# Weight conversion moved off GpSimd, first-group squares on ScalarE, natural rows for w_in: a linear-attention and feed-forward kernel on one core

## The chip, the cores and the metric

The kernel runs on one core of a Trainium2 chip. The core has five engines that work side by side and wait for each other by semaphores: TensorE (PE, matrix products, with its weight loads shown as PEld), VectorE (DVE), ScalarE (ACT), GpSimd (POOL) and SyncE (SP), which here only issues DMAs. The metric is the time of one execution in device microseconds (us), as the median of several runs.

## The reference

Four batches of eight heads, 768 steps, head size 48. A state of 48x48 per head decays and takes up an outer product at each step; the rows of the result, all heads side by side, then go through a feed-forward block.

```python
for t in range(S):                       # (B, H, S, D) = (4, 8, 768, 48)
    state = alpha[:, :, t, :, None] * state + einsum('bhd,bhe->bhde', k[:, :, t], v[:, :, t])
    y[:, :, t] = einsum('bhd,bhde->bhe', q[:, :, t], state)
x = y.transpose(0, 2, 1, 3).reshape(B * S, H * D)      # 3072 x 384
h = np.maximum(x @ w_in, 0.0)                          # w_in 384 x 2048
out = (h * h) @ w_out                                  # w_out 2048 x 384
```

q, k, v and alpha are fp32. w_in and w_out come as 64-bit floats, two 32-bit words each, and become fp32 on the chip, by bit operations on the words.

## The kernel before

The tokens are cut into 24 blocks of 128 steps (six chunks of four batches). The attention of a block has four stages, named in the code: `decays` (transposes of alpha on PE, logarithm on ACT, running sum on DVE, two exponentials on ACT), `turn` (q and k transposed and scaled), `scores` (q times k per head, masked by DVE; k turned back), and `values` (state update, and y in PSUM). Every four blocks make a group of 512 tokens. Its y lands in a tile xT of 3 x 128 rows, model dimension on the partitions, which is read by the feed-forward part: `ffn_in` makes one of 16 hidden slices of 128 (three steps over xT, relu on ACT, square on DVE), `ffn_out` adds two hidden slices into the output tile of one block (PE), and copies the tile out at the end.

The order of all instructions is written by hand: each engine takes its own in the order of the code. First comes a prelude, the attention of blocks 0 to 3. Then, for each group g, there are 16 slots; a slot holds one attention stage of the blocks of group g+1 and the next units of feed-forward work of group g, two `ffn_in` units in each of the first eight slots, four `ffn_out` units in each of the last eight. So the attention of the next group runs between the matmuls of this one. Group 5 has no attention beside it.

The weights come in 16 pieces of 128 x 768 (eight of w_in, eight of w_out), through three raw tiles. `next_weights`, called three times in the prelude and once or twice a slot in group 0, converts one piece and issues the load of another. A piece takes one ACT instruction (L133), five on DVE (L134 to L149) and two on POOL (L152, L153). The state product is also on POOL (L283).

The head size 48 is not a divisor of 128. So the heads lie in pairs, at partitions 0 to 47 and 64 to 111 of four tiles. Before, xT keeps that layout for three of the four pairs, and the last pair goes into the gaps (partitions 48 to 63 and 112 to 127) by six small DMAs (L296), and w_in is loaded with its rows in the same arrangement, by four DMAs a piece on SP's and ACT's queues (L113, L114).

SP and ACT issue their DMAs in program order, and an issue waits for a semaphore that an earlier DMA still holds; there are eight, used in turn.

Of the kernel before, what the change touches and what calls it, by code (L numbers as in the profile page):

```python
# [8 lines left out]
FP32 = mybir.dt.float32  # L9
U32 = mybir.dt.uint32  # L10
AF = mybir.ActivationFunctionType
ALU = mybir.AluOpType
PSUM = bass.MemoryType.PSUM
# [6 lines left out]
def kernel(  # L20
# [30 lines left out]
    NJ = DF // 128  # L51
    G = 64 - D
    NR = 3
    assert S % C == 0 and H * D == DM and NP == KM + 1 and KM * G == D and NBLK % GB == 0

    consts = ctx.enter_context(tc.tile_pool(name="consts", bufs=1))
    raw_pool = ctx.enter_context(tc.tile_pool(name="raw", bufs=NR))
# [2 lines left out]
    p2 = ctx.enter_context(tc.tile_pool(name="p2", bufs=2))  # L60
    x_pool = ctx.enter_context(tc.tile_pool(name="x", bufs=2))
    ps_att = ctx.enter_context(tc.tile_pool(name="ps_att", bufs=4, space=PSUM))
    ps_h = ctx.enter_context(tc.tile_pool(name="ps_h", bufs=2, space=PSUM))
    ps_o = ctx.enter_context(tc.tile_pool(name="ps_o", bufs=2, space=PSUM))
    ctx.enter_context(tc.manual_schedule())


# [35 lines left out]
    def load_weights(i):  # L103
        dst = (w_in + w_out)[i]
        dt = moe_w_in.dtype
        raw = dst if dt == FP32 else raw_pool.tile(list(dst.shape), dt, tag="raw", name="raw")
        raws[i] = raw
        if i < NW:
            src = moe_w_in[:, i * DF // NW : (i + 1) * DF // NW]
            own = src[0 : 2 * KM * D].rearrange("(k e r) f -> r e k f", e=2, r=D)  # L110
            gap = src[2 * KM * D : DM].rearrange("(e k r) f -> r e k f", e=2, r=G)
            for e, dma in enumerate((nc.sync, nc.scalar)):
                dma.dma_start(out=raw[64 * e : 64 * e + D], in_=own[:, e])  # L113
                dma.dma_start(out=raw[64 * e + D : 64 * e + 64], in_=gap[:, e])  # L114
        else:
            i -= NW
            src = moe_w_out[i * DF // NW : (i + 1) * DF // NW, :]
            nc.sync.dma_start(out=raw, in_=src.rearrange("(j r) m -> r j m", r=128))

    def convert_weights(i):  # L120

        if moe_w_in.dtype == FP32:
            return
        w = (w_in + w_out)[i].rearrange("a k f -> a (k f)")
        n = w.shape[1]
        words = raws.pop(i).rearrange("a k f -> a (k f)").bitcast(U32)
        words = words.rearrange("a (n h) -> a n h", h=2)
        lo, hi = words[:, :, 0], words[:, :, 1]  # L130
        mag = cv_pool.tile([128, n], U32, tag="mag", name="mag")
        cut = cv_pool.tile([128, n], U32, tag="cut", name="cut")
        nc.scalar.activation(out=w, in_=lo, func=AF.Copy, scale=2.0**-52)  # L133
        nc.vector.tensor_scalar(  # L134
            out=mag, in0=hi, scalar1=1, scalar2=None, op0=ALU.logical_shift_left
        )
        nc.vector.tensor_scalar(  # L137
            out=cut, in0=hi, scalar1=3, scalar2=0x3FFFFFF8,
            op0=ALU.logical_shift_left, op1=ALU.bitwise_and,
        )  # L140
        nc.vector.scalar_tensor_tensor(  # L141
            out=cut, in0=hi, scalar=0xC0000000, in1=cut,
            op0=ALU.bitwise_and, op1=ALU.bitwise_or,
        )
        nc.vector.scalar_tensor_tensor(  # L145
            out=cut.bitcast(FP32), in0=mag, scalar=float(897 << 21), in1=cut.bitcast(FP32),
            op0=ALU.is_ge, op1=ALU.mult,
        )
        nc.vector.tensor_scalar(  # L149
            out=mag, in0=cut, scalar1=0xFF800000, scalar2=None, op0=ALU.bitwise_and  # L150
        )
        nc.gpsimd.tensor_tensor(out=w, in0=w, in1=mag.bitcast(FP32), op=ALU.mult)  # L152
        nc.gpsimd.tensor_tensor(out=w, in0=w, in1=cut.bitcast(FP32), op=ALU.add)  # L153

    for n in range(NIN):
        load(n)
    to_load, to_convert = list(range(2 * NW)), list(range(2 * NW))

    def next_weights():
        if to_convert:  # L160
            convert_weights(to_convert.pop(0))
        if to_load:
            load_weights(to_load.pop(0))


# [5 lines left out]
    again = consts.tile([128, NP, C], FP32, name="again")  # L171
    nc.vector.memset(again, 1.0)
    nc.vector.memset(again[:, :, 0:1], 0.0)
    NAM = 2
    am_t = kept("am", NAM, [128, 2, NP, 128])
    for t in am_t:
# [62 lines left out]
    def values(n):  # L239
        c, batch = divmod(n, B)  # L240
        qT = qkT.pop(n)[0]
        b = bs.pop(n)
        v_in = tiles["v"][n % NV]
        am = am_t[n % NAM]
        st = s_t[batch]
        kv = None
        if c < NCH - 1:
            kv = ps_att.tile([128, NP, 2 * D], FP32, tag="att", name="kv")
            kt = ks.pop(n)
            for p in range(NP):  # L250
                nc.tensor.matmul(  # L251
                    out=kv[:, p, :], lhsT=kt[:, p, :],
                    rhs=v_in[:, 2 * p * D : 2 * (p + 1) * D], start=True, stop=True,
                )
            sm = p2.tile([128, NP, D], FP32, tag="sm", name="sm")
            for e in range(2):
                rows = slice(64 * e, 64 * e + D)
                new = kv[rows, :, e * D : (e + 1) * D]
                if c == 0:
                    nc.vector.tensor_copy(out=sm[rows], in_=new)  # L260
                else:
                    nc.vector.tensor_tensor(  # L262
                        out=sm[rows], in0=new, in1=st[rows, :, 64 * e : 64 * e + D], op=ALU.add
                    )

        y = ps_att.tile([128, NP, C], FP32, tag="att", name="y")
        if c:
            for p in range(NP):
                nc.tensor.matmul(  # L269
                    out=y[:, p, :], lhsT=st[:, p, :], rhs=qT[:, p, :],  # L270
                    start=(p == 0), stop=False, skip_group_check=True,
                )
        for p in range(NP):
            for e in range(2):
                nc.tensor.matmul(  # L275
                    out=y[64 * e : 64 * e + 64, p, :], lhsT=v_in[:, (2 * p + e) * D : (2 * p + e) * D + 64],
                    rhs=am[:, e, p, :], start=(c == 0 and p == 0), stop=True,
                    skip_group_check=True,
                )
        if kv is not None:  # L280
            for e in range(2):
                rows = slice(64 * e, 64 * e + D)
                nc.gpsimd.tensor_tensor(  # L283
                    out=st[rows, :, 64 * e : 64 * e + D], in0=sm[rows],
                    in1=b[rows, :, C - 1 : C].to_broadcast([D, NP, D]), op=ALU.mult,
                )
        g, t = divmod(n, GB)
        if t == 0:
            xT[g] = x_pool.tile([128, KM, GB * C], FP32, tag="xT", name="xT")
        x = xT[g][:, :, t * C : (t + 1) * C]  # L290
        yg = p2.tile([128, C], FP32, tag="yg", name="yg")
        nc.scalar.activation(out=yg, in_=y[:, KM, :], func=AF.Copy)  # L292
        nc.scalar.activation(out=x, in_=y[:, 0:KM, :], func=AF.Copy)
        for e in range(2):
            for kk in range(KM):
                nc.sync.dma_start(  # L296
                    out=x[64 * e + D : 64 * e + 64, kk, :],
                    in_=yg[64 * e + G * kk : 64 * e + G * (kk + 1), :],
                )


    hid, acc = {}, {}

    def ffn_in(g, j):
        hid[j] = hid_pool.tile([128, GB * C], FP32, tag="hid", name="hid")
        w, c0 = w_in[j * NW // NJ], j % (NJ // NW) * 128
        ps = ps_h.tile([128, GB * C], FP32, tag="h", name="h")
        for kk in range(KM):
            nc.tensor.matmul(  # L309
                out=ps, lhsT=w[:, kk, c0 : c0 + 128], rhs=xT[g][:, kk, :],  # L310
                start=(kk == 0), stop=(kk == KM - 1),
            )
        r = p2.tile([128, GB * C], FP32, tag="r", name="r")
        nc.scalar.activation(out=r, in_=ps, func=AF.Relu)  # L314
        nc.vector.tensor_tensor(out=hid[j], in0=r, in1=r, op=ALU.mult)  # L315

    def ffn_out(g, t, i):
        per = NJ // NW
        if i == 0:
            acc[t] = ps_o.tile([128, 512], FP32, tag="o", name="o")  # L320
        for j in range(per * i, per * (i + 1)):
            nc.tensor.matmul(  # L322
                out=acc[t][:, 0:DM],
# [19 lines left out]
    for n, s in order:  # L343
# [5 lines left out]
        if s == 3 and n + NV == GB:  # L349
            load(n + NV)  # L350
            load_weights(to_load.pop(0))
        if n == GB - 1 and s > 0:
            next_weights()

    NS = GB * len(stages)
    for g in range(NBLK // GB):
        units = [(ffn_in, (g, j)) for j in range(NJ)]
        units += [(ffn_out, (g, t, i)) for t in range(GB) for i in range(NW)]
        cost = {ffn_in: KM * GB * C, ffn_out: NJ // NW * DM}
        total = sum(cost[f] for f, _ in units)  # L360
        done = 0
        for slot in range(NS):
            i, s = divmod(slot, len(stages))
            n = (g + 1) * GB + i
            if n < NBLK:
                stages[s](n)
            for _ in range(1 + s % 2):
                next_weights()
            if s == 0 and n + 1 < NBLK:
                load(n + 1)  # L370
            while units and done * NS < total * (slot + 1):
# [33 lines left out]
```

## Time and profile before

| | |
|---|---|
| median of 3 runs | 722.15 us (721.2 to 723.8) |
| the profiled execution, its span | 723.61 us, 721.8 us |
| PE busy | 659.7 us (91%) |
| PE weight load | 387.0 us (54%) |
| DVE busy | 268.7 us (37%) |
| ACT busy | 149.5 us (21%) |
| POOL busy | 92.3 us (13%) |
| granted PE clock, mean | 0.955 |

Busy times are sums over the span. They say which engine has the most to do, and nothing on where it waits; a stage with its own limit shows only when the span is cut into windows. A matmul of the program stands in the trace as two records (fp32 goes through PE twice), so a unit of `ffn_in` is six records.

### The profile page before, as it was taken

The numbers are of one execution on the slowest core, as the hardware profiler recorded it, in microseconds if no ns is written. First come the engines' busy times: TensorE is split into PE (matmuls) and PEld (weight loads), VectorE is DVE, ScalarE is ACT, GpSimd is POOL, SyncE is SP. The second block draws the span as 40 slices with busy tenths as digits, with TensorE's granted clock in tenths as the row PEclk, the third lists the DMA queues.
The fourth block names the chain that finished last, engine by engine and source line by source line (L and its number), as shares of the span: only waits on it lengthen the run. The fifth ranks groups of instructions, "written<-read, shape, count | busy, mean of one in ns | idle before, by whom it ended". The sixth has DMA issues, their size and how long they took to land.

```text
span 721.8 us, 7282 instructions
## 1 busy us (share of the span) xinstructions
PE 659.7 (91%) x2800; PEld 387.0 (54%) x2800; DVE 268.7 (37%) x344; ACT 149.5 (21%) x277; POOL 92.3 (13%) x93
## 2 busy tenths in 40 slices
PE   4685765867999999999999999999999999999998
PEld 2562432434665556665456665556665456644554
DVE  3479999992114331114331113421213421112100
ACT  1233223310112221112320122320122221112100
POOL 1036655651000000000000000000000000000000
PEclk9877996985999999999999999999999999999999
DMA  9955835320302312311320321330330230000000
GB/s 157 152 94 124 142 124 121 114 41 11 58 14 55 47 24 35 59 35 34 47 40 18 67 44 16 48 46 12 68 58 3 44 48 25 11 15 0 1 22 22
DMA packets 113698, 37.83 MB, mean 52 GB/s; under 512 B 103168, under 2 KB 108544, under 8 KB 113664
## 3 DMA queue, kind: packets, MB, share of 16 engines
q1 hardware_dynamic: 111872, 34.23, 25.8%
q10 hardware_dynamic: 1792, 3.15, 2.3%
q8 instruction: 22, 0.36, 0.2%
q14 instruction: 12, 0.10, 0.1%
HBM read 31.46 MB, written 4.72 MB: 50 GB/s over the span
## 4 chain that ended last, share of the span: by engine, by line
PE 79%; DVE 13%; SPq 3%; DMA 3%; issue 1%; POOL 1%; ACT 0%; ACTq 0%; DVEq 0%; POOLq 0%
PE o L322 34%; PE h L309 30%; PE sc L221 3%; PE y L275 3%; DVE hid L315 3%; DVE cut L141 2%; SPq L93 2%; PE y L269 2%; PE kv L251 2%; DVE cut L145 2%; DMA raw<-in_moe_w_in_dram 2%; DVE cut L137 2%; PE kT L186 1%; DVE mag L134 1%; PE kr L235 1%
## 5 line engine op out<-in xcount | busy, mean ns | idle before, releaser
L309 PE MATMUL h<-xT,w_in 128*128 128x512 f32 x576 | 262.4, 608 | 23.7 <-ACT r L314 15.7
L322 PE MATMUL o<-w_out,hid 128*128 128x384 f32 x768 | 261.0, 495 | 11.5 <-POOL w_out L153 11.5
L322 PEld LDWEIGHTS o<-w_out,hid 128*128 128x128 f32 x768 | 144.4, 193 | 108.0 <-POOL w_out L153 13.9
L309 PEld LDWEIGHTS h<-xT,w_in 128*128 128x128 f32 x576 | 108.6, 195 | 149.7 <-issue 139.0
L315 DVE TENSOR_TENSOR hid<-r 128x512 f32<-128x512 f32 x96 | 78.5, 825 | 176.0 <-ACT r L314 175.9
L314 ACT ACTIVATE r<-h 128x512 f32<-128x512 f32 x96 | 56.8, 595 | 177.6 <-PE h L309 158.3
L283 POOL TENSOR_TENSOR s<-sm,b 48x192 f32<-48x192 f32 x40 | 23.3, 581 | 381.0 <-PE y L269 346.8
L196 DVE TENSOR_TENSOR_SCAN la<-again,la 128x512 f32<-128x512 f32 x24 | 32.4, 1352 | 92.7 <-ACT la L194 92.7
L227 DVE COPY_PREDICATED am<-causal,sc 128x512 f32<-128x512 uint32 x48 | 32.3, 726 | 55.0 <-PE sc L221 54.9
L330 ACT ACTIVATE osb<-o 128x384 f32<-128x384 f32 x24 | 11.8, 490 | 166.8 <-PE o L322 166.8
L275 PE MATMUL y<-am,v_in 128*64 128x128 f32 x384 | 30.5, 302 | 4.2 <-DVE am L227 4.2
L221 PEld LDWEIGHTS sc<-qT,kT 48*128 48x128 f32 x384 | 25.4, 202 | 14.6 <-issue 13.1
L221 PE MATMUL sc<-qT,kT 48*128 48x128 f32 x384 | 30.2, 300 | 0.0
L292 ACT ACTIVATE yg<-y 128x128 f32<-128x128 f32 x24 | 6.6, 277 | 112.0 <-PE y L275 104.8
L212 DVE TENSOR_TENSOR qT<-qT,b 128x512 f32<-128x512 f32 x24 | 16.5, 690 | 35.0 <-PE qT L186 30.0
L262 DVE TENSOR_TENSOR sm<-kv,s 48x192 f32<-48x192 f32 x32 | 11.3, 353 | 45.3 <-PE kv L251 44.8
L203 ACT ACTIVATE b<-la 128x512 f32<-128x512 f32 x24 | 15.1, 630 | 62.6 <-DVE la L196 62.6
L275 PEld LDWEIGHTS y<-am,v_in 128*64 128x64 f32 x384 | 23.5, 149 | 7.8 <-DVE am L227 5.1
L251 PEld LDWEIGHTS kv<-v_in,ks 128*128 128x128 f32 x160 | 22.3, 205 | 8.0 <-issue 3.8
L186 PE MATMUL qT<-ident,q_in 128*128 128x128 f32 x96 | 15.9, 292 | 9.7 <-ACT la L194 9.7
L251 PE MATMUL kv<-v_in,ks 128*128 128x96 f32 x160 | 22.7, 289 | 1.0 <-ACT ks L237 1.0
L186 PEld LDWEIGHTS qT<-ident,q_in 128*128 128x128 f32 x96 | 12.6, 150 | 19.1 <-ACT la L194 10.3
(42 smaller groups left out, 365.7 us busy)
## 6 DMA issues: line engine op xcount, KB each, us to landing
raw<-in_moe_w_out_dram SPq DMA_DIRECT2D x8, 768.0 KB, 4.4
a_in<-in_alpha_dram SPq DMA_DIRECT2D x24, 192.0 KB, 3.3
q_in<-in_q_dram SPq DMA_DIRECT2D x24, 192.0 KB, 3.9
k_in<-in_k_dram SPq DMA_DIRECT2D x24, 192.0 KB, 4.4
v_in<-in_v_dram SPq DMA_DIRECT2D x24, 192.0 KB, 4.4
out_dram<-osb SPq DMA_DIRECT2D x24, 192.0 KB, 1.9
raw<-in_moe_w_in_dram ACTq DMA_DIRECT2D x8, 288.0 KB, 5.2
raw<-in_moe_w_in_dram SPq DMA_DIRECT2D x8, 288.0 KB, 5.2
```

The lines of the kernel that those rows point to most:

```text
L186: nc.tensor.transpose(out=ps[:, p, :], in_=rows[:, 128 * p : 128 * (p + 1)], identity=ident)
L196: nc.vector.tensor_tensor_scan(out=la.rearrange("a p t -> a (p t)"), data0=again.rearrange("a p t -> a (p t)"), data1=la.rearrange("a p t ...
L212: nc.vector.tensor_tensor(out=t, in0=ps, in1=factor, op=ALU.mult)
L221: nc.tensor.matmul(out=ps[e][:, p, :], lhsT=kT[rows, p, :], rhs=qT[rows, p, :], start=True, stop=True,)
L227: nc.vector.copy_predicated(out=am_t[n % NAM][:, e], mask=causal.bitcast(U32).unsqueeze(1).to_broadcast([128, NP, C]), data=ps[e],)
L251: nc.tensor.matmul(out=kv[:, p, :], lhsT=kt[:, p, :], rhs=v_in[:, 2 * p * D : 2 * (p + 1) * D], start=True, stop=True,)
L275: nc.tensor.matmul(out=y[64 * e : 64 * e + 64, p, :], lhsT=v_in[:, (2 * p + e) * D : (2 * p + e) * D + 64], rhs=am[:, e, p, :], start=(c = ...
L283: nc.gpsimd.tensor_tensor(out=st[rows, :, 64 * e : 64 * e + D], in0=sm[rows], in1=b[rows, :, C - 1 : C].to_broadcast([D, NP, D]), op=ALU.mult,
L309: nc.tensor.matmul(out=ps, lhsT=w[:, kk, c0 : c0 + 128], rhs=xT[g][:, kk, :], start=(kk == 0), stop=(kk == KM - 1),)
L314: nc.scalar.activation(out=r, in_=ps, func=AF.Relu)
L315: nc.vector.tensor_tensor(out=hid[j], in0=r, in1=r, op=ALU.mult)
L322: nc.tensor.matmul(out=acc[t][:, 0:DM], lhsT=hid[j][:, t * C : (t + 1) * C], rhs=w_out[i][:, j % per, :], start=(j == 0), stop=(j == NJ - 1),)
```

## The change

- Conversion: per piece two DVE instructions that split exponent and upper mantissa (`convert_first`), two on ACT (the exponent shifted by a relu with a bias, the lower word), and, one call later, three on DVE (`convert_second`: sign, mantissa, product). POOL has none. The first call stands one stage earlier, and there is one call per slot in group 0 instead of one or two.
- The state product stands on DVE.
- In group 0, the squares are on ACT, and the `ffn_out` units go by weight piece (all four blocks with piece 0, then with piece 1, ...), not by block. Hidden and output tiles share four PSUM banks.
- xT has natural rows: y is copied as a whole to a tile ys and moved to xT by ten DMAs of 16, 32 or 48 rows on SP's queue. w_in is loaded by one DMA a piece on SP's queue.

```diff
-            for e, dma in enumerate((nc.sync, nc.scalar)):
-                dma.dma_start(out=raw[64 * e : 64 * e + D], in_=own[:, e])
-                dma.dma_start(out=raw[64 * e + D : 64 * e + 64], in_=gap[:, e])
+            nc.sync.dma_start(out=raw, in_=src.rearrange("(k r) f -> r k f", r=128))
...
+    def convert_first(i):
...
+        nc.vector.tensor_scalar(
+            out=power, in0=hi, scalar1=20, scalar2=0x7FF,
+            op0=ALU.logical_shift_right, op1=ALU.bitwise_and,
         )
         nc.vector.tensor_scalar(
+            out=upper, in0=hi, scalar1=0xFFFFF, scalar2=None, op0=ALU.bitwise_and
+        )
+        nc.scalar.activation(
+            out=power, in_=power, func=AF.Relu, scale=2.0**23, bias=rebias
+        )
+        nc.scalar.activation(out=w, in_=lo, func=AF.Copy, scale=2.0**-52, bias=1.0)
+        half[i] = w, hi, power, upper
+
+    def convert_second(i):
+        w, hi, power, upper = half.pop(i)
         nc.vector.scalar_tensor_tensor(
+            out=power, in0=hi, scalar=0x80000000, in1=power,
             op0=ALU.bitwise_and, op1=ALU.bitwise_or,
         )
         nc.vector.scalar_tensor_tensor(
+            out=w, in0=upper, scalar=2.0**-20, in1=w, op0=ALU.mult, op1=ALU.add
+        )
+        nc.vector.tensor_tensor(out=w, in0=w, in1=power.bitcast(FP32), op=ALU.mult)
-        nc.gpsimd.tensor_tensor(out=w, in0=w, in1=mag.bitcast(FP32), op=ALU.mult)
-        nc.gpsimd.tensor_tensor(out=w, in0=w, in1=cut.bitcast(FP32), op=ALU.add)
...
+            if i < 2 * NW:
+                convert_first(i)
+            if 0 < i <= 2 * NW:
+                convert_second(i - 1)
+        if i and to_load:
             load_weights(to_load.pop(0))
...
+            for old, new, last in pieces:
+                nc.vector.tensor_tensor(out=old, in0=new, in1=last, op=ALU.mult)
...
+        ys = p2.tile([128, NP, C], FP32, tag="ys", name="ys")
+        nc.scalar.activation(out=ys, in_=y, func=AF.Copy)
+        for h in range(H):
+            p, e = divmod(h, 2)
+            d = 0
+            while d < D:
+                kk, r = divmod(h * D + d, 128)
+                m = min(D - d, 128 - r)
                 nc.sync.dma_start(
+                    out=xT[g][r : r + m, kk, t * C : (t + 1) * C],
+                    in_=ys[64 * e + d : 64 * e + d + m, p, :],
                 )
+                d += m
...
-        nc.vector.tensor_tensor(out=hid[j], in0=r, in1=r, op=ALU.mult)
+        if g == 0:
+            nc.scalar.activation(out=hid[j], in_=r, func=AF.Square)
+        else:
+            nc.vector.tensor_tensor(out=hid[j], in0=r, in1=r, op=ALU.mult)
...
+        outs = [(g, t, i) for t in range(GB) for i in range(NW)]
+        units += [(ffn_out, a) for a in (outs if g else sorted(outs, key=lambda a: a[2]))]
...
-            for _ in range(1 + s % 2):
-                next_weights()
+            next_weights()
```

ACT's queue in the prelude, from block 0's first exponential to block 2's logarithm; before (`la` holds the logarithms, `yg` and `xT` the copies of y):

```order
L203 ACTIVATE b<-la 128x512
L205 ACTIVATE inv<-la 128x512
L113 DMA raw<-in_moe_w_in_dram 48x3x256
L114 DMA raw<-in_moe_w_in_dram 16x3x256
L113 DMA raw<-in_moe_w_in_dram 48x3x256
L114 DMA raw<-in_moe_w_in_dram 16x3x256
L194 ACTIVATE la<-aT 128x512
```

And now:

```order
L208 ACTIVATE b<-la 128x512
L210 ACTIVATE inv<-la 128x512
L199 ACTIVATE la<-aT 128x512
L208 ACTIVATE b<-la 128x512
L210 ACTIVATE inv<-la 128x512
L242 ACTIVATE ks<-kr 128x512
```

The weight loads are gone from between block 0's exponentials and block 1's logarithm; they stand on SP's queue.

DVE in the second slot of group 0 (`turn` of block 4); before:

```order
L315 TENSOR_TENSOR hid<-r 128x512 x2
L212 TENSOR_TENSOR qT<-qT,b 128x512
L212 TENSOR_TENSOR kT<-kT,inv 128x512
L134 TENSOR_SCALAR mag<-raw 128x768
L137 TENSOR_SCALAR cut<-raw 128x768
L141 SCALAR_TENSOR_TENSOR cut<-raw,cut 128x768
L145 SCALAR_TENSOR_TENSOR cut<-mag,cut 128x768
L149 TENSOR_SCALAR mag<-cut 128x768
```

And now (`w_in_119` is the fifth piece, converted in two calls):

```order
L217 TENSOR_TENSOR qT<-qT,b 128x512
L217 TENSOR_TENSOR kT<-kT,inv 128x512
L128 TENSOR_SCALAR power<-raw 128x768
L132 TENSOR_SCALAR upper<-raw 128x768
L143 SCALAR_TENSOR_TENSOR power<-raw,power 128x768
L147 SCALAR_TENSOR_TENSOR w_in_119<-upper,w_in_119 128x768
L150 TENSOR_TENSOR w_in_119<-w_in_119,power 128x768
```

The squares are gone from DVE, before this slot had a second conversion of the same five instructions behind the first, and the two instructions that end a piece, once on POOL, are within DVE's five.

SP's queue where a group ends; before, in group 1 and later:

```order
L296 DMA xT<-yg 16x128 x6
L333 DMA out_dram<-osb 128x384
L93 DMA a_in_84<-in_alpha_dram 128x8x48
L93 DMA q_in_87<-in_q_dram 128x8x48
L93 DMA k_in_90<-in_k_dram 128x8x48
```

And now (the first such place, with the four outputs of group 0 behind it):

```order
L299 DMA xT<-ys 48x128 x2
L299 DMA xT<-ys 32x128
L299 DMA xT<-ys 16x128
L299 DMA xT<-ys 48x128 x2
L299 DMA xT<-ys 16x128
L299 DMA xT<-ys 32x128
L299 DMA xT<-ys 48x128 x2
L340 DMA out_dram<-osb 128x384 x4
```

Ten issues stand where six stood, ahead of the outputs and of the next block's loads.

## Rows read from the trace of the kernel before

**Rows 1.** Windows, groups 0 and 1: us, busy PE, PEld, DVE, ACT, POOL, clock, DMA, GB/s.

```profile
61.60:215.50 153.90, 122.34 (x480) 69.67 (x481) 108.39 (x111) 32.86 (x57) 63.93 (x36) 0.85 0.37 82
215.50:322.00 106.50, 106.50 (x482) 63.42 (x481) 28.80 (x44) 22.98 (x45) 4.07 (x8) 1.00 0.22 40
```

**Rows 2.** Timeline, PE's first h matmuls: start, duration, instruction, count, idle before.

```profile
61.68 8.40 PE L309 MATMUL h<-xT,w_in 128*128 128x512 f32 x12 [8.01 <-DMA xT<-yg]
```

**Rows 3.** Groups of instructions, 60 to 165 us: count, busy, mean ns, idle before, releasers.

```profile
L309 PE MATMUL h<-xT,w_in 128*128 128x512 f32 x96 | 49.9, 676 | 23.7 <-ACT r L314 15.7 <-DMA xT<-yg 8.0
L315 DVE TENSOR_TENSOR hid<-r 128x512 f32<-128x512 f32 x16 | 23.2, 1490 | 0.0
...
L141 DVE SCALAR_TENSOR_TENSOR cut<-raw,cut 128x768 uint32<-128x768 uint32 x14 | 19.9, 1424 | 0.5
...
L137 DVE TENSOR_SCALAR cut<-raw 128x768 uint32<-128x768 uint32 x13 | 14.2, 1096 | 0.0
...
L322 PE MATMUL o<-w_out,hid 128*128 128x384 f32 x28 | 11.3, 547 | 6.0 <-POOL w_out L153 6.0
L314 ACT ACTIVATE r<-h 128x512 f32<-128x512 f32 x16 | 9.2, 594 | 28.6 <-DVE hid L315 10.5 <-PE h L309 9.4 <-PE kv L251 4.7
...
L133 ACT ACTIVATE w_out<-raw 128x768 f32<-128x768 uint32 x8 | 7.1, 911 | 0.0
```

**Rows 4.** The same instructions where POOL rests: timeline before 46 us, groups of group 1.

```profile
44.34 0.56 DVE L137 TENSOR_SCALAR cut<-raw 128x768 uint32<-128x768 uint32 x1
44.93 0.96 DVE L141 SCALAR_TENSOR_TENSOR cut<-raw,cut 128x768 uint32<-128x768 uint32 x1
...
L315 DVE TENSOR_TENSOR hid<-r 128x512 f32<-128x512 f32 x16 | 11.1, 692 | 33.6 <-ACT r L314 33.6
```

**Rows 5.** Timeline of the prelude: PE's transposes, ACT, one load of ACT, one of SP.

```profile
8.32 1.11 PE L186 MATMUL aT<-ident,a_in 128*128 128x128 f32 x4 [1.07 <-DMA a_in<-in_alpha_dram]
...
18.32 1.03 SPq L93 DMA_DIRECT2D v_in<-in_v_dram  x1
18.70 0.60 ACT L194 ACTIVATE la<-aT 128x512 f32<-128x512 f32 x1 [10.60 <-DMA k_in<-in_k_dram]
...
26.13 0.93 PE L186 MATMUL aT<-ident,a_in 128*128 128x128 f32 x4
...
30.52 0.32 ACTq L114 DMA_DIRECT2D raw<-in_moe_w_in_dram  x1
30.89 0.60 ACT L194 ACTIVATE la<-aT 128x512 f32<-128x512 f32 x1 [3.99 <-DMA raw<-in_moe_w_in_dram]
...
54.54 0.49 ACT L293 ACTIVATE xT<-y 128x384 f32<-128x384 f32 x1
```

**Rows 6.** Timeline where group 0 ends and group 1 begins: ACT, SP, PE.

```profile
209.94 0.28 ACT L292 ACTIVATE yg<-y 128x128 f32<-128x128 f32 x1 [7.38 <-PE y L275]
...
210.63 3.67 SPq L296 DMA_DIRECT2D xT<-yg  x6
...
215.53 5.32 PE L309 MATMUL h<-xT,w_in 128*128 128x512 f32 x12
```

**Rows 7.** Instructions of tile xT, 200 to 700 us: ns min/median/max, first and last start.

```profile
L296 SPq DMA_DIRECT2D xT<-yg x102: 512/582/1132, 210.6 to 634.5; - x102
...
DMA to landing us min/median/max: 1.6/1.7/2.6
```

**Rows 8.** Line 93, loads of q, k, v and alpha: ns min/median/max, first and last start.

```profile
L93 SPq DMA_DIRECT2D a_in<-in_alpha_dram x24: 384/482/1112, 0.7 to 584.8; - x24
...
L93 SPq DMA_DIRECT2D v_in<-in_v_dram x24: 794/966/2001, 2.5 to 586.7; - x24
```

**Rows 9.** Timeline, PE after a short and a long idle time.

```profile
79.44 5.39 PE L309 MATMUL h<-xT,w_in 128*128 128x512 f32 x12 [1.67 <-ACT r L314]
...
150.12 1.46 PE L322 MATMUL o<-w_out,hid 128*128 128x384 f32 x4
...
159.16 2.93 PE L322 MATMUL o<-w_out,hid 128*128 128x384 f32 x4 [5.31 <-POOL w_out L153]
```

## Prediction before the run

> **What bounds the kernel now.** I read the stages by window first, then the groups of instructions of the first stage, then the timeline of the places where TensorE (PE) waits. The windows by feed-forward group [rows 1] show two different kernels. From 215.5 us on, a group takes 106.5 us and PE is busy for all of it at granted clock 1.00, the level of 2.4 GHz; three groups in a row read like the one shown. No other engine matters there unless it makes PE wait. Group 0 (61.6 to 215.5) takes 153.9 us for the same matmuls: PE 122.3 busy at clock 0.85, VectorE (DVE) 108.4, GpSimd (POOL) 63.9. So 47.4 us is what group 0 can lose at most, and what lies ahead of its first h matmul at 61.68 [rows 2] comes on top.
>
> Why group 0 is slow is in its groups of instructions [rows 3]. Before h PE idled 23.7 us, mostly behind the ACT relu, which waited for DVE squares to free its tile; before o it idled 6.0 us, for the POOL add that ends a weight conversion. The squares took 1490 ns each, the conversion's and/or step 1424 ns, its shift 1096 ns. The same instructions while POOL rests: square 692, and/or 0.96 us, shift 0.56 us [rows 4]. So DVE runs up to twice as long beside POOL's weight products, and PE waits for the two of them.
>
> Ahead of group 0 the timeline of ScalarE (ACT) shows two gaps that compute does not explain [rows 5]: block 1's transposes end at 9.43 (8.32+1.11), its logarithm starts at 18.70; block 2's end at 27.06, its logarithm starts at 30.89. Between them ACT has w_in loads to issue (the one at 30.52 stands just ahead), and the trace names DMAs as releasers. Less the 0.07 that a logarithm takes to start, that is 9.2 and 3.8 us.
>
> **The change, part by part.**
>
> *A. Start of group 0.* The w_in loads leave ACT's queue, so both logarithms follow their transposes, and nothing on ACT stands between. Of the end of block 3's eviction of y, 55.03 (54.54+0.49, rows 5), I take off 13.0: 42.0. Second, y now goes by ten DMAs instead of six. One such issue had 0.58 us as its median, and six took 3.67, so 0.62 from one to the next [rows 6, 7]; the tenth starts 5.6 after the first and lands 1.7 later, at 49.3. Third, all of that is on SP's queue, which may be later than the data: SP ends its sixteenth block load at 19.35 (18.32+1.03), then come two weights (0.5 each, like the cheapest load), ten y issues (6.2), four loads of block 4 (between 0.48 and 0.97 each [rows 8], 2.9), a weight, 6.2, 6.2, two weights, and the last ten to landing (7.3): 50.7. I take 51. It is 57 if half of the 13.0 comes back elsewhere: DVE does 4 us of the first conversions ahead of block 3's mask copy, and a y issue can wait for the landing of the weight load just ahead of it, since in the new program the issues take eight semaphores in turn. The six matmuls of slot 0 took 8.40 us, where six at full clock take 5.32 [rows 2, 6]. After the last slice of xT four of them are left: 3.5 to 5.6 us and a slow beginning, 5.2. Slot 0 ends at 56.2 instead of 70.1 (61.68+8.40). Gain 13.9, bounds 8 and 17.
>
> A rule of the Trainium skill speaks against this part. "DMA: Bandwidth & Descriptors", section "Issuing engines are not separate DMA queues", says that issuing from several engines saves only the sequencer's issue time. By it, what ACT gets back is issuing alone, four issues of 0.32 in the prelude's two gaps, 1.3 us, and A would shrink to 2.2. The row shows ACT idle for 10.6 us ahead of one logarithm, with a DMA as what it waited for, so a wait and not issuing is what ACT lost here.
>
> *B. Slots 1 to 15 of group 0.* Conversion on DVE was five instructions a piece and two POOL products. Now it is two shift/mask ones of 0.56, two two-tensor ones of 0.96 [rows 4], and an fp32 product of 768. The product has no row: 692 ns for 512 is the nearest, so between 0.69 and 1.04; I take 0.96, as the other two-operand instruction of 768. Sum 4.0, 4.1 with gaps. Attention adds per four slots a scan, two products, two mask copies and four small state steps. I price these from the steady windows: 28.8 us of DVE per group, less 16 squares of 692 = 11.1 [rows 1, 4], gives 17.7 for 16 slots, 1.1 a slot; the state products that leave POOL are two small ones every four slots, so 1.4 a slot at most. DVE: 5.5 a slot. ACT gains the exponent step (911 ns, priced as the other conversion of 768) and two squares (594 each as the relu) [rows 3]: 1.8 + 2.4 + 0.8 for the rest (22.98 a group less 16 relus of 0.594, over 16 slots [rows 1]) = 5.0 a slot. PE needs 106.5/16 = 6.66. So both stay below PE, and with POOL silent nothing stretches DVE. Conversions come one a slot, last one in slot 12, each at least two slots ahead of its use; the outputs part by part need one w_out piece a slot instead of all eight in slots 8 and 9. Hidden cover: DVE 1.1 us a slot; were DVE at 7.5 instead of 5.5, twelve slots would cost 10 more.
>
> Slots 1 to 15 took 145.4 (70.08 to 215.53, rows 2 and 6); a steady group without two h units takes 106.5 - 5.3 = 101.2. I add 4: 1 for each block's scan, behind which ACT holds its relus, most of it covered by four shared PSUM banks, and 0.6 where the four output copies of group 0 come together and two of them wait for an output DMA. Gain 40.2, bounds 28 and 44.
>
> *C. Group boundaries.* Here the change takes something back. The last y of a group is copied at 209.94, six DMAs follow at 210.63, and h starts at 215.53 with no idle time [rows 6]. Now one copy of 128x512 (about 0.6, as the two before together), then ten issues. The first feed-forward matmul reads xT in three steps of 128 rows, 0.89 apart (5.32/6). Rows 0 to 127 need DMAs 1 to 3, the next 4 to 7, the last 8 to 10. The tenth starts at 210.6 + 5.6 = 216.2 and lands at 217.9; it is wanted at 217.3 (215.53 + 2 x 0.89). Stall 0.6, four times, and about 1.0 before group 5, where no transposes stand ahead of h: 3.4. If an issue of 48 rows is cheaper (0.51, the least) there is none; at 0.8 it is 2.3 a boundary, 12. The squares of later groups stay on DVE, and the state products moved there fall into its 77.7 idle us of 106.5 [rows 1]: nothing. The shared PSUM pool changes nothing for groups 1 to 5, where PE is never without a bank today.
>
> **Sum.** 13.9 + 40.2 - 3.4 = 50.7. The profiled execution took 723.6 (span 721.8 and 1.8 around it): 672.9. It was 1.5 above the median of the runs, 722.15, so 671.5; I say 672.
>
> **Rivals.**
>
> 1. *DVE still paces group 0.* If an instruction of the new chain is dearer than its neighbours (unsigned input to a multiply-add, bit operations in place), DVE takes 7.5 a slot and the 4 us of slack in B become 14: 682. For it: DVE is the fullest engine after PE, and ACT now waits for DVE in the middle of a conversion. Against: 0.96 holds for both two-operand forms of before.
> 2. *The start stays late.* If ACT lost only the 1.3 us of issuing ahead of its two logarithms, and the rest of the 13.0 was time in which data were not there yet, A gives 13.9 - 13.0 + 1.3 = 2.2: 683. For it: the loads are as many bytes as before, and SP's queue has 16 more issues of y. Against: block 1's alpha had been transposed at 9.43, so the logarithm's data were there. It is what the section of the Trainium skill named above would have.
> 3. *SP's issues are dear: slower than before.* One mechanism, the ten issues. Every 0.1 us per issue above 0.62 costs 4.0 us ahead of group 0 (40 issues) and 0.9 at each of five boundaries: 8.5 us. From 0.6 above, that is 1.2 us per issue, the whole 50.7 is gone, and at 1.3 it is 729. The loads of v have 0.97 in the median [rows 8], and one y issue took 1.13 [rows 7]. If a boundary's wait grows to 5 us the clock goes too: after 1.67 us of idling PE ran twelve records of h in 5.39, about its best, but after 5.31 us four records of o took 2.93, against 1.46 a little earlier [rows 9]. Against: 0.58 is the median of 102.
> 4. *No boundary stall and a quick start*: the ten issue at 0.51 each, A gives 17 and B 43: 662.
>
> That the change does not do what it says: POOL has no instruction left after its first memsets and masks in the new order, so this is small.
>
> **How the numbers follow.** Forecast (667 to 677) 0.515; rival 1 0.16; rival 2 0.13; rival 4 0.14; rival 3's mechanism at 0.8 to 0.95 us per issue, 687 to 700, 0.02; at about 1.2, no change, 0.01; above, slower, 0.025. The range takes in rivals 1, 2 and 4 and some us beyond them, since two can meet: 658 to 692; the likeliest case's own is 667 to 677. Faster by over 0.3% 0.965, within 0.3% (about what a measurement of this kernel can tell from no change) 0.01, slower 0.025.
>
> **What would show it.** A: the logarithms of blocks 1 and 2 directly behind their transposes, and the first h at 48 to 52. B: the window from there to group 1's first h 108 to 116 long, DVE's steps at 0.56 and 0.96 throughout, PE hardly waiting for ACT or weights. C: a PE wait for xT of 0.5 to 1 us at 161, 268 and so on, and y issues of 0.6. I would be wrong by a DVE instruction well above 1 us, by a first h after 57, or by boundary waits of over 2 us.

## The result and the profile after

The changed kernel took 675.65 us (median of 4 runs, 675.14 to 676.14) against 721.67 of the kernel before beside it: ratio 0.9361, 95% interval 0.9334 to 0.9388. The profiled execution has a span of 674.1 us, 47.7 less than before. Cut at the same places as the prediction:

| stretch | before, us | after, us | gain | predicted |
|---|---|---|---|---|
| A: start to the end of slot 0's matmuls | 70.1 | 61.1 | 8.9 | 13.9 |
| B: from there to group 1's first h | 145.4 | 101.2 | 44.3 | 40.2 |
| C: from there to the end | 506.3 | 511.8 | -5.5 | -3.4 |

Windows of the changed kernel (columns as in [rows 1]): slots 1 to 15 of group 0, and group 1.

```profile
61.10:162.30 101.20, 101.20 (x469) 61.04 (x468) 62.64 (x93) 47.20 (x71) 0.00 (x0) 1.00 0.47 112
162.30:269.70 107.40, 106.62 (x481) 63.22 (x480) 31.43 (x52) 23.17 (x42) 0.00 (x0) 1.00 0.27 50
```

PE is busy for all of the first at clock 1.00. The 101.2 us are what a steady group takes for the same slots, so nothing is left to gain there while PE has these matmuls to do. In the second, 0.8 us of PE's time is idle, where [rows 1] had none.

Groups of instructions of the changed kernel, 60 to 165 us; these answer to [rows 3]:

```profile
L313 PE MATMUL h<-xT,w_in 128*128 128x512 f32 x92 | 41.4, 595 | 0.8 <-DMA xT<-ys 0.8
...
L143 DVE SCALAR_TENSOR_TENSOR power<-raw,power 128x768 uint32<-128x768 uint32 x12 | 11.4, 948 | 0.0
L135 ACT ACTIVATE power<-power,rebias 128x768 uint32<-128x768 uint32 x11 | 10.2, 930 | 5.9 <-DVE power L128 5.9
...
L150 DVE TENSOR_TENSOR w_out<-w_out,power 128x768 f32<-128x768 f32 x8 | 7.7, 958 | 0.3
...
L128 DVE TENSOR_SCALAR power<-raw 128x768 uint32<-128x768 uint32 x11 | 6.0, 547 | 0.1
```

DVE's steps have the lengths of [rows 4] throughout: 0.55 for a shift, 0.95 for a two-operand step, and 0.96 for the product that had no row. PE waits for none of them.

Timeline of the prelude, to be read beside [rows 5]: both logarithms now start 0.03 us behind their transposes.

```profile
8.53 1.12 PE L191 MATMUL aT<-ident,a_in 128*128 128x128 f32 x4 [1.04 <-DMA a_in<-in_alpha_dram]
...
9.68 0.60 ACT L199 ACTIVATE la<-aT 128x512 f32<-128x512 f32 x1 [1.42 <-PE aT L191]
...
15.88 0.66 PE L191 MATMUL aT<-ident,a_in 128*128 128x128 f32 x4
...
16.57 0.60 ACT L199 ACTIVATE la<-aT 128x512 f32<-128x512 f32 x1
```

And the end of the prelude, up to the first h (before: [rows 2]): SP's y DMAs and weight loads, block 3's y on PE and its copy on ACT.

```profile
18.83 9.02 SPq L299 DMA_DIRECT2D xT<-ys  x10
...
32.02 13.57 SPq L299 DMA_DIRECT2D xT<-ys  x20
...
33.59 2.48 PE L280 MATMUL y<-am,v_in 128*64 128x128 f32 x16 [0.23 <-DVE am L232]
...
40.67 0.60 ACT L292 ACTIVATE ys<-y 128x512 f32<-128x512 f32 x1 [1.09 <-DMA xT<-ys]
...
45.68 1.07 SPq L109 DMA_DIRECT2D raw<-in_moe_w_in_dram  x2
46.84 8.28 SPq L299 DMA_DIRECT2D xT<-ys  x10
...
53.60 7.54 PE L313 MATMUL h<-xT,w_in 128*128 128x512 f32 x12 [16.49 <-DMA xT<-ys]
...
56.46 0.29 PEld L313 LDWEIGHTS h<-xT,w_in 128*128 128x128 f32 x1 [0.67 <-DMA xT<-ys]
```

SP's queue is full from 17 to 55 us. Block 3's y was computed by 36.1 us (33.59+2.48) and copied to ys by 41.27 (40.67+0.60), but its DMAs are issued from 46.84 on, and PE idles 16.5 us. The row at 56.46 is the weight load of the third of slot 0's six matmuls: it waits for the last slice of xT. The chain of waits of that stretch has two landings in it (start, duration, what):

```profile
18.15 7.89 DMA raw<-in_moe_w_in_dram
...
48.77 4.86 DMA xT<-ys
```

Block 0's ten issues took 9.02 instead of 6.2, because one of them waited for the semaphore of a weight load that landed 7.89 us after its start. The y copy of block 3 that releases the first h landed 4.86 us after its issue, just behind two weight loads; 1.8 is the median.

A group's end, as in [rows 6]:

```profile
156.73 0.60 ACT L292 ACTIVATE ys<-y 128x512 f32<-128x512 f32 x1 [7.38 <-PE y L280]
157.35 6.22 SPq L299 DMA_DIRECT2D xT<-ys  x10
...
162.31 1.88 PE L313 MATMUL h<-xT,w_in 128*128 128x512 f32 x4
...
164.97 3.67 PE L313 MATMUL h<-xT,w_in 128*128 128x512 f32 x8 [0.78 <-DMA xT<-ys]
```

Ten issues take 6.22 us, and h stops after its first two steps over xT until the last copies land: 0.78 us idle. The twelve records around this wait take 6.33 us (162.31 to 168.64), where they took 5.32 [rows 6]: 1.01 more, of which only the 0.78 shows as idle.

### The profile page after: what moved, and what is told of

Same layout as the page of the kernel before. It is cut to its first block, busy times and chain, and to the rows that moved or that the text cites. A ratio compares the mean times of both kernels' runs of the same rounds, so it can differ in the third digit from the quotient of the medians.

```text
span 674.1 us, 7156 instructions
## 1 busy us (share of the span) xinstructions
PE 641.4 (95%) x2800; PEld 376.6 (56%) x2800; DVE 233.4 (35%) x361; ACT 172.3 (26%) x285; POOL 2.6 (0%) x21
## 4 chain that ended last, share of the span: by engine, by line
PE 86%; SPq 7%; DMA 4%; ACT 1%; issue 1%; ACTq 0%
PE h L313 36%; PE o L329 33%; SPq L299 6%; PE sc L226 4%; PE y L280 3%; PE y L274 3%; DMA xT<-ys 2%; PE kv L256 2%; PE kr L240 2%; PE qT L191 1%; PE kT L191 1%; DMA raw<-in_moe_w_in_dram 1%; PE aT L191 1%; DMA a_in<-in_alpha_dram 1%; SPq L92 1%
## 5 line engine op out<-in xcount | busy, mean ns | idle before, releaser
L313 PE MATMUL h<-xT,w_in 128*128 128x512 f32 x576 | 259.1, 599 | 20.3 <-DMA xT<-ys 20.3
L329 PE MATMUL o<-w_out,hid 128*128 128x384 f32 x768 | 255.7, 488 | 0.0
L313 PEld LDWEIGHTS h<-xT,w_in 128*128 128x128 f32 x576 | 106.4, 191 | 144.7 <-issue 125.8
L322 DVE TENSOR_TENSOR hid<-r 128x512 f32<-128x512 f32 x80 | 55.3, 692 | 172.9 <-ACT r L318 172.9
L201 DVE TENSOR_TENSOR_SCAN la<-again,la 128x512 f32<-128x512 f32 x24 | 29.3, 1222 | 78.0 <-ACT la L199 78.0
L292 ACT ACTIVATE ys<-y 128x512 f32<-128x512 f32 x24 | 14.3, 596 | 97.6 <-PE y L280 96.5
L226 PEld LDWEIGHTS sc<-qT,kT 48*128 48x128 f32 x384 | 24.1, 193 | 13.9 <-issue 13.1
L217 DVE TENSOR_TENSOR qT<-qT,b 128x512 f32<-128x512 f32 x24 | 16.5, 690 | 34.8 <-PE qT L191 33.8
L280 PE MATMUL y<-am,v_in 128*64 128x128 f32 x384 | 27.5, 284 | 0.3 <-DVE am L232 0.2
L274 PE MATMUL y<-qT,s 128*128 128x128 f32 x160 | 21.5, 278 | 0.0
L191 PE MATMUL aT<-ident,a_in 128*128 128x128 f32 x96 | 16.0, 294 | 5.1 <-DMA a_in<-in_alpha_dram 5.1
L135 ACT ACTIVATE power<-power,rebias 128x768 uint32<-128x768 uint32 x16 | 14.9, 930 | 23.2 <-DVE power L128 23.2
```

What stands on the lines that cost most here:

```text
L191: nc.tensor.transpose(out=ps[:, p, :], in_=rows[:, 128 * p : 128 * (p + 1)], identity=ident)
L201: nc.vector.tensor_tensor_scan(out=la.rearrange("a p t -> a (p t)"), data0=again.rearrange("a p t -> a (p t)"), data1=la.rearrange("a p t ...
L226: nc.tensor.matmul(out=ps[e][:, p, :], lhsT=kT[rows, p, :], rhs=qT[rows, p, :], start=True, stop=True,)
L274: nc.tensor.matmul(out=y[:, p, :], lhsT=st[:, p, :], rhs=qT[:, p, :], start=(p == 0), stop=False, skip_group_check=True,)
L280: nc.tensor.matmul(out=y[64 * e : 64 * e + 64, p, :], lhsT=v_in[:, (2 * p + e) * D : (2 * p + e) * D + 64], rhs=am[:, e, p, :], start=(c = ...
L313: nc.tensor.matmul(out=ps, lhsT=w[:, kk, c0 : c0 + 128], rhs=xT[g][:, kk, :], start=(kk == 0), stop=(kk == KM - 1),)
```

## The experiments

The ratios are to the kernel before, on the same chip.

**1. w_in on SP's queue alone, in the kernel before.**

```diff
-            for e, dma in enumerate((nc.sync, nc.scalar)):
+            for e, dma in enumerate((nc.sync, nc.sync)):
```

> The kernel before, with its four w_in loads per piece all on SP's queue and none on ACT's. Theory (ACT waited in its own queue for the DMA semaphores): the logarithms of blocks 1 and 2 start right behind their transposes (9.5 and about 18 instead of 18.70 and 30.89 us), the first h starts 8 to 13 us before 61.68, group 0 stays at about 154 us, total 709 to 715. Rival (issuing on two queues only saves issue time): the logarithms stay where the data come, total 720 to 725.

710.71 us, ratio 0.9847 (0.9819 to 0.9875). Its timeline:

```profile
9.49 0.60 ACT L194 ACTIVATE la<-aT 128x512 f32<-128x512 f32 x1 [1.40 <-PE aT L186]
...
16.56 0.60 ACT L194 ACTIVATE la<-aT 128x512 f32<-128x512 f32 x1
...
56.47 3.75 PE L309 MATMUL h<-xT,w_in 128*128 128x512 f32 x4 [19.46 <-DMA xT<-yg]
```

The logarithms stand where the theory put them, and as many DMAs are issued as before. What ACT lost was a wait: an issue on ACT's queue, held by a DMA's semaphore, holds ACT's computing behind it. In the kernel before, it is the third of the four issues ahead of block 1's logarithm (the one that ends the order of ACT's queue before):

```profile
9.50 0.32 ACTq L114 DMA_DIRECT2D raw<-in_moe_w_in_dram  x1
...
17.84 0.32 ACTq L113 DMA_DIRECT2D raw<-in_moe_w_in_dram  x1
```

The first h comes 5.2 us earlier, less than the 8 to 13 expected; group 0 gave the rest, 148.7 us (56.5 to 205.2) instead of 153.9.

The Trainium skill ("DMA: Bandwidth & Descriptors", "Issuing engines are not separate DMA queues") has issuing time as all that a second engine's queue saves. This run shows that such a queue can also cost: 10.6 us ahead of block 1's logarithm [rows 5], where the four issues themselves (0.32 to 0.45 each) are 1.5.

**2 and 3. Squares back on DVE, without and with the last product on POOL.** In the changed kernel:

```diff
-        if g == 0:
+        if g < 0:
             nc.scalar.activation(out=hid[j], in_=r, func=AF.Square)
```
```diff
-        nc.vector.tensor_tensor(out=w, in0=w, in1=power.bitcast(FP32), op=ALU.mult)
+        nc.gpsimd.tensor_tensor(out=w, in0=w, in1=power.bitcast(FP32), op=ALU.mult)
```

The first edit alone:

> The changed kernel with the squares of group 0 on DVE as before, nothing else. DVE then has about 6.9 us a slot for eight slots against PE's 6.66. Theory (DVE unstretched nearly keeps up): 675 to 680, squares at 0.69 us. Rival (moving the squares to ACT was what let group 0 run at PE's rate): PE waits for relu and squares in group 0, 684 or more.

675.06 us, ratio 0.9361 (0.9341 to 0.9381). The squares' move to ACT is worth nothing in this kernel. Both edits:

> The changed kernel with two edits: the squares of group 0 back on DVE, and the last product of a conversion on POOL instead of DVE. Compared with the run that has the squares edit alone, DVE has 16 instructions of 0.96 us less to do. Theory (DVE is stretched while POOL works): shifts and and/or steps beside a POOL product take 1.1 to 2.4 us instead of 0.56 and 0.95, squares up to 1.5 us, group 0 is 8 to 20 us longer than 100, total 682 to 695. Rival (only the amount of work on DVE counts): durations as in the changed kernel, total no more than the squares edit alone.

676.25 us, ratio 0.9373 (0.9351 to 0.9395): on the time the theory is wrong, and the rival right within the intervals. On the durations neither is. Its groups of instructions, 60 to 165 us:

```profile
L322 DVE TENSOR_TENSOR hid<-r 128x512 f32<-128x512 f32 x16 | 23.0, 1472 | 1.7 <-ACT r L318 1.2
...
L150 POOL TENSOR_TENSOR w_out<-w_out,power 128x768 f32<-128x768 f32 x8 | 14.5, 1814 | 37.4 <-DVE w_out L147 37.4
L143 DVE SCALAR_TENSOR_TENSOR power<-raw,power 128x768 uint32<-128x768 uint32 x12 | 11.4, 948 | 0.0
...
L128 DVE TENSOR_SCALAR power<-raw 128x768 uint32<-128x768 uint32 x11 | 6.0, 547 | 0.7 <-POOL w_out L150 0.6
```

Only the squares are stretched; shifts and two-operand steps are not. And 1472 ns is a mean of two kinds of square, as its timeline shows:

```profile
59.88 1.80 POOL L150 TENSOR_TENSOR w_in<-w_in,power 128x768 f32<-128x768 f32 x1 [2.88 <-DVE w_in L147]
59.97 2.26 DVE L322 TENSOR_TENSOR hid<-r 128x512 f32<-128x512 f32 x1 [0.17 <-ACT r L318]
...
62.54 0.69 DVE L322 TENSOR_TENSOR hid<-r 128x512 f32<-128x512 f32 x1 [0.32 <-ACT r L318]
```

POOL's product comes at the end of a conversion, and what DVE does next is a square. The one that starts beside the product takes 2.26 us and ends 0.55 behind it; the next, with POOL idle, takes 0.69. So an instruction is stretched that falls beside a POOL one, not the engine as a whole, and DVE still kept up with PE. Whether such an instruction is slowed or held until POOL is done was not tested.

**4 to 6. What made group 0 slow in the kernel before.** Run 4 takes the pace alone from the change (the shared banks and the order of the outputs belong to it; the first conversion stands where it stood, and one call is added in the prelude, behind block 2's `values`):

```diff
+    ps_ffn = ctx.enter_context(tc.tile_pool(name="ps_ffn", bufs=GB, space=PSUM))
...
+        outs = [(g, t, i) for t in range(GB) for i in range(NW)]
+        units += [(ffn_out, a) for a in (outs if g else sorted(outs, key=lambda a: a[2]))]
...
-        if n == GB - 1 and s > 0:
+        if n == GB - 1 and s > 0 or (n, s) == (GB - 2, 3):
...
-            for _ in range(1 + s % 2):
-                next_weights()
+            next_weights()
```

> The kernel before with the new pace alone: one conversion per slot and one call earlier, group 0's outputs by weight piece, four shared PSUM banks; conversions with POOL, squares on DVE, w_in through ACT's queue and the old layout as before. Theory (the bursts and the block-wise outputs cost part of group 0, DVE stretched by POOL the rest): DVE has 9.4 us a slot for eight slots and 6.4 for four against PE's 6.66, group 0 is 120 to 130 us instead of 154, total 692 to 702. Rival (POOL's stretching alone makes group 0 slow): total 715 or more.

Run 5 is run 4 with group 0's squares on ACT (`if g == 0: nc.scalar.activation(out=hid[j], in_=r, func=AF.Square)`).

> The run with the new pace in the kernel before, and group 0's squares on ACT as well; POOL still ends each conversion. Theory: DVE has 6.4 us a slot against PE's 6.66, so group 0 runs within 10 us of PE's rate and the total is 676 to 688, with the late start of before left. Rival (POOL's chain and its stretching of DVE hold the weights back in any pace): 695 or more.

Run 6 leaves the two POOL instructions (L152, L153) out of the kernel before.

> The kernel before without the two POOL instructions that end a conversion (the weights then lack their upper part), everything else as it was. DVE's work is the same. Theory (POOL's products stretch DVE): shifts 0.56, and/or 0.96, squares 0.69 us throughout, DVE's busy time in group 0 falls from 108 to 70 to 80 us, total 685 to 700. Rival (DVE's own amount of work in the bursts is the limit): DVE busy over 95 us, total 715 or more.

| | total, us | ratio (95% interval) | first h to group 1's first h, us |
|---|---|---|---|
| before, beside runs 4 to 6 | 723.06 | 1 | 153.9 [rows 1] |
| run 4, new pace | 695.63 | 0.9625 (0.9601 to 0.9648) | 119.7 |
| run 5, pace and squares on ACT | 688.91 | 0.9533 (0.951 to 0.9556) | 113.0 |
| run 6, without L152 and L153 | 682.24 | 0.9443 (0.9415 to 0.947) | 113.6 |
| changed kernel | 675.65 | 0.9361 (0.9334 to 0.9388) | 108.7 |

On the total, run 4 falls in the range expected, run 5 is one us above its own, run 6 three us below. Runs 4 and 5 reach their first h 5.4 and 5.7 us later than the kernel before, which was not followed; so their totals gain less than group 0 does. The windows of group 0 (columns as in [rows 1]) of runs 4, 5 and 6:

```profile
67.10:186.80 119.70, 111.88 (x481) 66.23 (x481) 100.72 (x106) 31.69 (x54) 61.39 (x35) 0.94 0.44 95
```

```profile
67.40:180.40 113.00, 110.51 (x481) 65.78 (x482) 92.44 (x90) 41.71 (x70) 58.97 (x35) 0.96 0.48 100
```

```profile
60.80:174.40 113.60, 109.96 (x481) 64.66 (x482) 70.87 (x107) 31.96 (x55) 4.49 (x8) 0.97 0.49 108
```

DVE has the same instructions in run 6 as before, and 70.9 us busy where [rows 1] has 108.4: the stretching is worth 37.5 us of DVE. In run 4 DVE is still stretched (100.7 busy), and yet group 0 is 34 us shorter. In the kernel before, 31.6 us of group 0 were PE's idle time (153.9 less 122.3) and 15.8 were the lower clock (122.3 busy where a steady group has 106.5 [rows 1]). Run 4 has 7.8 and 5.4 of these, run 6 has 3.6 and 3.5: with the waits the clock's share goes too. So either cure alone gives 34 to 40 of the 45 us; they are not a sum.

Neither cure is a single thing. Run 4 changes the number of conversions a slot, the order of the outputs and the banks together. Run 6 takes out the stretching and also the two products as steps on the way to a weight, and PE waited for the second of them in the kernel before (its waits, 60 to 190 us: total, times, longest):

```profile
PE o L322 <- POOL w_out L153: 11.5, 3, 5.5
```

How the gain of each divides among these parts stays open. In run 5 the shift that stands beside POOL now is the one that suffers:

```profile
L136 DVE TENSOR_SCALAR cut<-raw 128x768 uint32<-128x768 uint32 x13 | 28.2, 2167 | 0.0
...
L140 DVE SCALAR_TENSOR_TENSOR cut<-raw,cut 128x768 uint32<-128x768 uint32 x13 | 13.2, 1018 | 0.4
```

2167 ns against 0.56 us in [rows 4], while the and/or step has 1018. In the kernel before, the shift's mean of 1096 [rows 3] hid the same two kinds (ns min/median/max):

```profile
L137 DVE TENSOR_SCALAR cut<-raw x13: 546/552/2178, 65.6 to 160.6; 128x768 uint32<-128x768 uint32 x13
```

**7. Twice as many y issues.** Each copy cut into two halves of its columns:

```diff
+                for c0 in (0, C // 2):
...
+                        out=xT[g][r : r + m, kk, t * C + c0 : t * C + c0 + C // 2],
+                        in_=ys[64 * e + d : 64 * e + d + m, p, c0 : c0 + C // 2],
```

> The changed kernel with each of the ten y DMAs cut into two of half the columns: twenty issues a block. Theory (SP's issue time is the price): ten more issues of 0.62 add 6.2 us at each of five group boundaries (from 0.8 to about 7, with some 3 us of slow clock behind such a wait) and 25 us ahead of the first h (53.6 to about 78); total 725 to 745, so slower than the kernel before. Rival (the DMAs' landing, not their issue, is waited for): boundaries stay under 2 us, total 676 to 690.

746.63 us, 1.6 above the range expected, ratio 1.0326 (1.0297 to 1.0355): slower than the kernel before. Its timeline at the first h and at group 1's first, then the windows (columns as in [rows 1]) from the end of that boundary's first wait on and of what follows:

```profile
73.50 2.04 PE L314 MATMUL h<-xT,w_in 128*128 128x512 f32 x2 [29.99 <-DMA xT<-ys]
77.92 2.04 PE L314 MATMUL h<-xT,w_in 128*128 128x512 f32 x2 [2.38 <-DMA xT<-ys]
81.66 5.92 PE L314 MATMUL h<-xT,w_in 128*128 128x512 f32 x8 [1.69 <-DMA xT<-ys]
```

```profile
189.06 1.10 PE L314 MATMUL h<-xT,w_in 128*128 128x512 f32 x2
194.21 2.05 PE L314 MATMUL h<-xT,w_in 128*128 128x512 f32 x2 [4.05 <-DMA xT<-ys]
198.09 5.73 PE L314 MATMUL h<-xT,w_in 128*128 128x512 f32 x8 [1.84 <-DMA xT<-ys]
```

```profile
194.20:203.90 9.70, 7.86 (x13) 3.10 (x14) 1.89 (x2) 3.15 (x7) 0.00 (x0) 0.59 0.48 127
203.90:290.00 86.10, 86.10 (x386) 50.66 (x386) 26.97 (x45) 18.57 (x33) 0.00 (x0) 1.00 0.23 37
```

PE waits 30.0 us ahead of h and twice more inside the first slot, and 5.9 us (4.05 and 1.84) at a boundary instead of 0.78. With these waits the clock goes as well, as rival 3 said: 0.59 granted at the boundary, 1.00 behind it, and two records of h take 2.05 us. The first h is 19.9 us later than in the changed kernel, group 1's first h 26.8, and the other 43 are lost at this boundary and the four behind it, 8 to 9 us each. So rival 3 had a real mechanism at a price that was not asked here: an issue takes 0.59, and it took twice as many of them to make the change a loss. 240 more issues cost 71 us (746.63 less 675.65).

**8 to 10. Another queue for the y copies.** In the changed kernel, every second head's copies on POOL (run 8) or ACT (run 9), or all on POOL (run 10):

```diff
-                nc.sync.dma_start(
+                (nc.sync, nc.gpsimd)[h % 2].dma_start(
```

> The changed kernel with every second head's y DMAs issued on POOL's queue, so five of ten per block leave SP. Theory (SP's queue, busy to 55 us, holds the start, and ten issues in a row hold each group boundary): 20 issues of 0.62 less ahead of the first h, which starts at 41 to 45 instead of 53.6, and the boundary waits of 0.8 us go; total 659 to 665. Rival (the start waits for weight landings and conversions, not for SP): first h at 51 or later, total 671 to 675.

> The changed kernel with every second head's y DMAs issued on ACT's queue. Theory (SP's queue is the limit of the start, and an issue on ACT that waits for a DMA semaphore holds ACT's own work, as in the kernel before): the boundary waits go (5 issues on each queue), but ACT's logarithms and relus wait in the prelude, so less is gained than on POOL (662.4): 664 to 672. Rival (any second queue is as good): 660 to 663.

> The changed kernel with all ten y DMAs of a block on POOL's queue, where an issue took 0.50 us and nothing else is queued. Theory (what is left of the late start, after half of the issues left SP, is the landing of the last y behind weight loads in the same DMA engines, 6 us): weight loads on SP go out earlier still, first h at 43 to 46, boundaries without waits of over 0.3 us, total 659 to 664. Rival (SP's remaining issues hold the start): first h at 41, total 656 to 658.

| | total, us | ratio (95% interval) | first h at, us |
|---|---|---|---|
| changed kernel | 675.65 | 0.9361 (0.9334 to 0.9388) | 53.60 |
| run 8, half on POOL | 662.41 | 0.9189 (0.9167 to 0.9211) | 46.02 |
| run 9, half on ACT | 669.6 | 0.9278 (0.9249 to 0.9307) | 52.60 |
| run 10, all on POOL | 660.19 | 0.9161 (0.9135 to 0.9187) | 42.37 |

Run 8 gains 13 us: 7.6 ahead of the first h, which is 1 us later than expected, and the rest behind it, where no boundary waits for y any more. The y issues of run 8 (ns min/median/max), and the landing that its chain of waits names ahead of h:

```profile
L299 POOL DMA_DIRECT2D xT<-ys x120: 494/502/634, 17.8 to 572.3; - x120
L299 SPq DMA_DIRECT2D xT<-ys x120: 509/584/1427, 19.1 to 572.5; - x120
```

```profile
39.98 6.05 DMA xT<-ys
```

Run 9 has no such waits either, but ACT's logarithms are late again, by 3.2 us each:

```profile
16.94 3.17 ACTq L299 DMA_DIRECT2D xT<-ys  x5
20.15 0.60 ACT L199 ACTIVATE la<-aT 128x512 f32<-128x512 f32 x1 [3.25 <-issue]
...
28.33 3.09 ACTq L299 DMA_DIRECT2D xT<-ys  x5
31.47 0.60 ACT L199 ACTIVATE la<-aT 128x512 f32<-128x512 f32 x1 [3.17 <-DMA xT<-ys]
```

So the first h is hardly earlier. The five issues in front take 3.17 and 3.09 us, 0.62 to 0.63 each, so at these two places ACT lost the issuing alone; the expectation had an issue that waits for a semaphore. The first h of run 10 is 0.6 us ahead of its range. POOL, which has nothing else to do here, helped as a second queue; ACT's queue cost ACT its own work.

**11 and 12. One weight load behind the y of block 3**, in the changed kernel and in run 8:

```diff
+            if (n, s) == (GB - 1, 3):
+                load_weights(to_load.pop(0))
-            next_weights()
+            next_weights(more=(n, s) != (GB - 1, 2))
```

> The changed kernel with the load of the fifth weight piece moved behind the ten y DMAs of block 3 (it stood ahead of them). Theory (the last y of the prelude lands late, 4.9 instead of 1.8 us, because two weight loads are just ahead of it): first h at 50 to 52 instead of 53.6, total 671 to 674. Rival (only the issues on SP count, and they are as many): no more than 0.5 us earlier, total 675 to 676.

673.51 us, ratio 0.934 (0.9316 to 0.9364); first h at 51.29 instead of 53.60. The landing that ends the wait, from its chain of waits:

```profile
48.64 2.67 DMA xT<-ys
```

It took 2.67 where the changed kernel had 4.86, and that is the gain at the first h: 2.2 of 2.3. On the total the intervals of the two overlap.

> Both edits together: every second head's y DMAs on POOL's queue and the fifth piece's load behind the y of block 3. Theory: first h at 42 to 44.5 instead of 46.0, total 658 to 661. Rival (the later weight holds group 0): 662 or more.

660.02 us, ratio 0.9153 (0.9131 to 0.9175); first h at 43.27. On top of run 8 the edit is worth 2.8 us at the first h. Run 12 beats both kernels, and run 10 is level with it within the intervals.

## Why the prediction came out right

The time came out 3.7 us above the 672 forecast, in the likeliest case's own range. That it came so close is in part luck: A fell 5.0 us short and C took 2.1 more than forecast, and B gave 4.1 back. The steps, in its order:

- *What bounds the kernel.* Right on the place: slots 1 to 15 of group 0 gave 44.3 of the 53.2 us gained, of which 5.5 went back at the boundaries. "Up to twice as long" was read off means: single instructions took up to four times, others were not touched. The [rows 3] end at 165 us, and up to there PE waited 6.0 us for POOL's add; over all of group 0 it was 11.5. The lower clock's 15.8 us were not counted by themselves.
- *A.* The mechanism was right, the size was not: 8.9 us for 13.9, the largest error of the sum. ACT's part came in full: block 3's y was copied by 41.27, with 42.0 forecast. The account of SP's queue was the right bound, but its 50.7 took every issue at 0.62. Block 0's ten took 9.02 and block 3's 8.28, since issues in both waited for a weight's semaphore (with one weight load later, in run 11, block 3's ten took 6.30). The tenth copy of block 3 was issued at 54.6 and landed at 56.4; from there to the end of slot 0 it was 4.7 us, with 5.2 forecast. The text named that wait as a risk and gave it to the far end, 57. That end is nearly what came, and the sum went by 51.
- *Rival 2* (and with it the section of the Trainium skill). Run 1 decided against: the wait on ACT was the issue held by a semaphore. Its price was miscounted: the two gaps hold six issues, 2.1 us, not four and 1.3; the verdict is the same.
- *B.* 44.3 for 40.2: the 4 us of slack was not needed at all. DVE's price (4.0 a piece) was right (0.547 + 0.551 + 2 x 0.948 + 0.958 = 3.95), the product's unknown 0.96 too. The count put the squares on ACT without a price for the move; it is worth nothing here (run 2). That DVE, stretched by POOL, is what made group 0 slow was half of the truth: the new pace or POOL's products taken out, either cure gives most of it (runs 4 and 6).
- *C.* -5.5 for -3.4. The wait was found where it was put, 0.7 to 0.9 us at each boundary where 0.6 to 1.0 was said, 3.8 in all, and an issue of 48 rows takes what one of 16 did. The other 1.7 lies at the same places: the records of h around a wait take longer than the idle time says (1.01 us for 0.78 at the first boundary). The sum had no term for that.
- *Rival 3* had a mechanism that is real, at a price that was not paid (run 7).

## What to carry to other kernels

Before putting many small copies on one queue, add up its issues in the order of the code, with the waits for the semaphores of slow transfers ahead: here 40 copies held the start, although the last block's y was copied 5.6 us, and computed 10.8, before the first of its DMAs was issued. Do not issue DMAs from an engine that computes something urgent: the issuing itself (run 9) and the wait for a semaphore (run 1) both hold its computing. When a stage has two causes of slowness, undo them one by one before adding their gains: here either cure alone gave 34 to 40 us of 45. And before reading a mean, look whether all instructions in it were slow.

## What the runs showed of the hardware

- Issuing a copy of y took 588 ns in the median on SP over the ten of 16, 32 and 48 rows, 582 for the six of 16 in [rows 7], and 502 on POOL: no dearer for the larger ones.
- A copy of y landed in 1.8 us in the median, but in 4.86 us behind two weight loads (the changed kernel), in 2.67 behind one (run 11), and in up to 8.10 (run 8).
- DVE instructions beside a POOL two-operand one took up to four times as long (2167 against 560 ns for a shift in run 5, 2.26 against 0.69 us for a square in run 3); the and/or step behind that shift took 1018 on average against 948.
